# The first feed-forward product with 512 columns instead of 480, the last 32 zeros

## The chip, the cores and the metric

The kernel runs on one core of one Trainium2 chip. The metric is the device time of one execution in microseconds (us); of the kernel before there are two runs, 1797.93 and 1798.88 us, with a median of 1798.41 us. Engines are named as the profile names them: PE is TensorE (PEld its weight loads), DVE is VectorE, ACT is ScalarE, POOL is GpSimd, SP is SyncE.

## The reference

```
x: (4, 12480, 128)   inducing: (32, 128)   w_in: (128, 2048)   w_out: (2048, 128)
def mab(q, kv):
    s = scale * (q @ kv.T);  s = s - s.max(-1)
    a = exp(s);  a /= a.sum(-1) + 1e-9
    return a @ kv
h = mab(inducing, x)             # per batch: 32 rows, from all 12480 tokens
y = mab(x, h)                    # each token over those 32 rows
r = max(y @ w_in, 0)
out = (r * r) @ w_out            # (49920, 128)
```

Two attentions per batch, and then a feed-forward with a squared ReLU. The bulk of the arithmetic is the feed-forward: 49,920 tokens through 128 x 2048 and 2048 x 128.

## The kernel before

**Tiling.** A batch has 13 units of 960 tokens, and a unit has two blocks of 480 tokens (`BLK`). The feed-forward runs block by block. Its 2048 hidden features are 16 tiles of 128, taken as 8 pairs, so there are 4 x 13 x 2 x 8 = 832 pairs in all.

**One pair.** `wide` (L508) makes the hidden features: two products, one for each tile of the pair, each with a weight tile of 128 x 128 (from `hw`, which is h @ w_in, made once per batch) and with `st` as the streamed operand. `st` holds the unnormalised attention weights of the block's 480 tokens, split into a high and a low part, on 128 partitions. The two results lie in `hp`, a PSUM tile of two banks of 512 float32 each, of which columns 0 to 479 are written. ACT reads those 480 columns of both banks (`relu`, L515, into `r`) and squares them (`square`, L522, into `g`). DVE or POOL rounds `g` to the shorter format fp32r (`high`, through `copy`, L593 or L595, into `hi`), and DVE subtracts (`low`, L530, into `lo`). Then `narrow` (L543) adds six products of 480 columns to the block's result `op`: hi with wo_hi, hi with wo_lo, lo with wo_hi, for both tiles. In one pair of each unit (marked "f" in the table `HI`) there is no split; it has two products in full float32 (`wo_f` with `g`). Both operands of `wide` are fp32r, as are those of the six narrow products.

**What makes `st`.** `second_unit` computes the second attention of the unit that comes next. Its last steps, `back(k)` (L477: four small products into a PSUM bank `ap`) and `stacked(k)` (L483 to L486), give `st` for block k: for k = 0 ACT copies `ap` to `st`, for k = 1 DVE does. `st` has four buffers. The other matrix work on PE is the first attention of the next batch (`xtp`, `sp`, `ep`, `hp` at L324), the scores (`s`, `s2t`) and the transposes of the output (`otp`).

**Order.** Nothing is scheduled by the tool chain: every step is put on one list with a position in time (`at(t, fn)`, the clock being pairs), the list is sorted, and the steps are emitted in that order. So each engine's queue follows the positions written in the kernel, and every engine takes its queue in order. POOL's queue holds the roundings `hi` that the table `HI` gives it (five in a unit), and three steps on `sk` (the split of the attention weights), of which the last copies the low part.

Of the kernel before, what the change touches and what calls it, by code (L numbers as in the profile page):

```python
# [11 lines left out]
F32 = mybir.dt.float32  # L12
F32R = mybir.dt.float32r
# [5 lines left out]
PSUM = bass.MemoryType.PSUM  # L19

P = 128
TS = 120          # tokens of a sub-tile
NT = 8            # sub-tiles of a unit
UNIT = TS * NT    # tokens of a unit
BLK = UNIT // 2   # tokens of a block, the width of the feed-forward products


@with_exitstack
def induced_attention_then_squared_relu_ffn(
# [8 lines left out]
    nc = tc.nc  # L38
    B, N, C = x.shape
# [3 lines left out]
    NP = NF // 2  # L43
    NU = N // UNIT
    Q = P // M
    scale = 1.0 / math.sqrt(C)
    # engines, by pair of f-tiles in the first and the second block of a unit; "f": not split
    SQ = ('aaaaaaaa', 'aaaaaaaa')   # of the square
    HI = ('vpvpvvpf', 'vvpvvpvv')   # of the rounding
    # engines that empty PSUM  # L50
    XT, XT_EARLY, ET, SS, ST, OT = 'av', 'aa', 'a', 'v', 'av', 'vv'
    RB, GB, HB, LB = 3, 4, 4, 3
    AT_G1, AT_SQA, AT_SQV, AT_HIP, AT_HIA, AT_HIV, AT_LO, AT_G2, AT_G2D = -1.4, 1.05, 0.8, 1.1, 0.7, 1.2, 2.05, 3.3, 0.16
# [17 lines left out]
    att = ctx.enter_context(tc.tile_pool(name="att", bufs=2))  # L71
# [5 lines left out]
    def bank(name):  # L77
        return ps_m.tile([P, 512], F32, tag="m", name=name)

    # token p * (N / TS) + j of a batch lies on partition p of sub-tile j  # L80
    x_v = x.rearrange("b (p j) c -> b p j c", p=TS)
    out_v = out.rearrange("(b p j) c -> b p j c", b=B, p=TS)

    def load_x(b, u, pool):
        xn = pool.tile([TS, NT, C], F32, tag="xn", name=f"xn_{b}_{u}")
        nc.sync.dma_start(xn, x_v[b, :, u * NT:(u + 1) * NT, :])
        return xn
# [4 lines left out]
    make_identity(nc, ident)  # L92
    identr = const.tile([P, P], F32R, name="identr")
    nc.vector.tensor_copy(identr, ident)
    # same_m[(q m), (k m')] = (m == m')
    same_m = const.tile([P, Q, M], F32, name="same_m")
    nc.vector.tensor_reduce(
        same_m[:, 0, :], ident.rearrange("p (q m) -> p m q", q=Q), axis=AX.X, op=ALU.add
# [2 lines left out]
        nc.vector.tensor_copy(same_m[:, k, :], same_m[:, 0, :])  # L101

    same = same_m.rearrange("p k m -> p (k m)")
    # lane_q[(q m), q'] = (q == q')
    lane_q = const.tile([P, Q], F32, name="lane_q")
    nc.vector.tensor_reduce(
        lane_q, ident.rearrange("p (q m) -> p q m", q=Q), axis=AX.X, op=ALU.add
# [6 lines left out]
    indT = const.tile([C, M], F32, name="indT")  # L114
    nc.vector.tensor_copy(indT, it_ps[:C, :M])

# [1 line left out]
    plan = []  # L118

    def at(t, fn):  # L120
        plan.append((t, len(plan), fn))
# [1 line left out]
    w_in_sb = const.tile([C, F], F32, name="w_in_sb")  # L123
    wo_hi = const.tile([P, NF, C], F32R, name="wo_hi")
    wo_lo = const.tile([P, NF, C], F32R, name="wo_lo")
    # w_out's tiles for the products that are not split
    FULL = [p for p in range(NP) if "f" in (HI[0][p], HI[1][p])]
    wo_f = const.tile([P, 2 * max(len(FULL), 1), C], F32, name="wo_f")

# [3 lines left out]
    ABOVE = float(np.array(1151 << 20, np.int32).view(np.float32))  # L133

    def weights(name, load, use, t0, step):
        """Steps that turn float64 weights, as words (low, high), into float32 parts (a, b).

        a has the leading 21 bits and b the rest; what float32 has no exponent for becomes 0 or
        infinite, as a cast would have it: a high word's order as a float32 is that of its exponent.
        """  # L140
        v = {}
        shape = [P, WCH]

        def tile_of(tag, dtype):
            return pools["stage"].tile(shape, dtype, tag=tag, name=f"{tag}_{name}")

        def words():
            v["w"] = pools["stage"].tile([P, WCH, 2], I32, tag="words", name=f"words_{name}")
            load(v["w"])

        def clamp():
            v["hc"] = tile_of("hc", F32)
            nc.vector.tensor_scalar(
                v["hc"], v["w"][:, :, 1].bitcast(F32), ABOVE, -ABOVE, ALU.min, ALU.max
            )

        def size():
            v["m"] = tile_of("m", F32)
            nc.scalar.activation(v["m"], v["hc"], AF.Abs)

        def flush():
            nc.vector.scalar_tensor_tensor(v["hc"], v["m"], LEAST, v["hc"], ALU.is_ge, ALU.mult)

        def field():
            v["a"] = tile_of("a", I32)
            nc.vector.tensor_scalar(
                v["a"], v["hc"].bitcast(I32), 3, 0x3FFFFFF8,
                ALU.logical_shift_left, ALU.bitwise_and,
            )

        def sign():
            nc.vector.scalar_tensor_tensor(
                v["a"], v["hc"].bitcast(I32), -0x40000000, v["a"], ALU.bitwise_and, ALU.bitwise_or
            )

        def power():
            v["power"] = tile_of("m", I32)
            nc.vector.tensor_single_scalar(v["power"], v["a"], -0x800000, ALU.bitwise_and)

        def low():  # L180
            v["b"] = tile_of("b", F32)
            nc.vector.scalar_tensor_tensor(
                v["b"], v["w"][:, :, 0].bitcast(U32), 2.0 ** -52, v["power"].bitcast(F32),
                ALU.mult, ALU.mult,
            )
            use(v["a"].bitcast(F32), v["b"])

        at(t0 - 1.5, words)
        for i, fn in enumerate((clamp, size, flush, field, sign, power, low)):
            at(t0 + step * i, fn)  # L190
# [4 lines left out]
        pools["stage"] = pools["scope"].enter_context(tc.tile_pool(name="stage", bufs=2))  # L195

    def open_ffn():
        """The feed-forward takes the place of the weights' staging."""
        pools["scope"].close()
        pools["ffn"] = ctx.enter_context(tc.tile_pool(name="ffn", bufs=3))  # L200

# [38 lines left out]

    state = {}

# [1 line left out]
    # lane (q m): inducing point m over the sub-tiles 2q and 2q + 1 of each unit  # L244
    def first_unit(b, u, t0, ahead, times, early=False):
        v = {}
        n = f"{b}_{u}"
        s = state.setdefault(b, {"xt": []})
# [4 lines left out]
        def turn(k):  # L253
# [8 lines left out]
            for t in range(4):  # L262
                nc.tensor.transpose(  # L263
                    tp[:, t * TS:(t + 1) * TS], v["xn"][:, 4 * k + t, :], ident[:TS, :TS]
                )
# [19 lines left out]
            nc.vector.tensor_reduce(v["mx"], v["sp"][:, :2 * TS], axis=AX.X, op=ALU.max)  # L285

        def shift():
            # the maximum so far, times -scale
            v["neg"] = tiny.tile([P, 1], F32, tag="neg", name=f"neg_{n}", bufs=4)
            if u:  # L290
                v["before"] = s["neg"]
                nc.vector.scalar_tensor_tensor(
                    v["neg"], v["mx"], -scale, s["neg"], ALU.mult, ALU.min
                )
            else:
                nc.vector.tensor_scalar_mul(v["neg"], v["mx"], -scale)
            s["neg"] = v["neg"]
# [50 lines left out]
            at(t0 + t, fn)  # L348

    def first_end(b, t0, times):  # L350
        """Joins the lanes of each inducing point; h transposed, four times, and h @ w_in split."""
        v = {}
        s = state[b]

# [50 lines left out]
        for t, fn in zip(times, fns):  # L405
            at(t0 + t, fn)

# [1 line left out]
    def second_unit(b, u, t0, times):  # L409
        """The unnormalised weights of a unit's tokens, split in two, as (hi, lo, hi, lo) on partitions."""  # L410
        v = {}
        n = f"{b}_{u}"
        s = state[b]
# [67 lines left out]
                )  # L481

        def stacked(k):  # L483
            st = att.tile([P, BLK], F32R, tag="st", name=f"st_{n}_{k}", bufs=4)
            copy(ST[k], st, v["ap"][:, :BLK])
            s["st", u, k] = st  # L486

        fns = (
# [3 lines left out]
        for t, fn in zip(times, fns):  # L492
            at(t0 + t, fn)

# [1 line left out]
    def ffn_block(b, u, k, t0):  # L496
        n = f"{b}_{u}_{k}"
        s = state[b]
        w = {}

        def pair(p):
            v = {}

            def wide(i):
                if i == 0:
                    v["hp"] = ps_h.tile([P, 2, 512], F32, tag="h", name=f"h_{n}_{p}")
                f = 2 * p + i
                nc.tensor.matmul(  # L508
                    v["hp"][:, i, :BLK], s["hw"][:, f * P:(f + 1) * P], s["st", u, k],
                    start=True, stop=True,  # L510
                )

# [60 lines left out]
        def turned():  # L573
            if k == 0:
                s["osb", u] = att.tile([TS, NT, C], F32, tag="osb", name=f"osb_{b}_{u}")
            # block k holds the sub-tiles 2q + k
            nc.vector.tensor_mul(  # L577
                s["osb", u].rearrange("t (q k) c -> t k q c", k=2)[:, k],
                w["tp"][:TS, :].rearrange("t (q c) -> t q c", q=Q),
                s["zz", u][:, k * Q:(k + 1) * Q].broadcast_to([TS, Q, C]),  # L580
            )
            if k == 1:
                nc.sync.dma_start(out_v[b, :, u * NT:(u + 1) * NT, :], s["osb", u])

# [4 lines left out]
    def copy(engine, dst, src):  # L589
        if engine == "a":  # L590
            nc.scalar.copy(dst, src)  # L591
        elif engine == "v":
            nc.vector.tensor_copy(dst, src)  # L593
        else:
            nc.gpsimd.tensor_scalar(dst, src, 1.0, 0.0, ALU.mult, ALU.add)  # L595

    # batch 0's first attention, then per batch its blocks and the first attention of the next
    U = 2 * NP
    t_end = START * NU + T_END
    t_main = t_end + T_FFN  # L600
# [52 lines left out]
```

## Time and profile before

| | |
|---|---|
| time, two runs | 1797.93 and 1798.88 us, median 1798.41 |
| span of the profiled execution | 1796.8 us; the runs' times are 1.1 to 2.1 us above it |
| mean granted clock of PE | 0.994 |
| PE busy | 1766.7 us, 98% |
| ACT busy | 1628.0 us, 91% |
| DVE busy | 1620.0 us, 90% |
| POOL busy | 442.8 us, 25% |
| share of PE in the chain that ended last | 95% |

The profiled execution's own time is not given apart from its span; its time lies with the two runs, its span plus one or two microseconds. In the page, a group row has the line, the engine, the operation, the operands with shapes, the count, then busy time and mean duration in ns, and the idle time of the engine before it. The rows of the timeline and of the chain begin with the start in us and the duration in us; "x2" means that two instructions are merged in the row. PE's durations contain the passage through the array, which overlaps the next product: what a product costs is read from the distance between starts. A float32 product appears as two records with the same operands, so the two float32 products of each of the 52 units are 208 records.

### The profile page before, as it was taken

What the parts mean: (1) busy time and instruction counts of PE and PEld (TensorE: products, weight loads), DVE (VectorE), ACT (ScalarE), POOL (GpSimd) and SP (SyncE); (2) the same over time, 40 slices, a digit from 0 to 9 for tenths busy, and PEclk for the clock granted to TensorE, in tenths of its full rate; (3) what the DMA queues carried; (4) which work ended last, traced back from release to release, by engine and by line L of the source; (5) the groups of instructions that cost most, each with busy time, mean ns of one, the idle gap of its engine ahead of it and who ended that gap; (6) DMA issues with size and microseconds to landing.
All of it is one profiled execution on the core that took longest, in us unless ns stands there. A gap on an engine that the chain in (4) does not pass through costs nothing.

```text
span 1796.8 us, 27067 instructions
## 1 busy us (share of the span) xinstructions
PE 1766.7 (98%) x9729; PEld 1422.9 (79%) x9729; DVE 1620.0 (90%) x2315; ACT 1628.0 (91%) x2070; POOL 442.8 (25%) x439
## 2 busy tenths in 40 slices
PE   7799999999999999999999999999999999999998
PEld 4478888888778888888878888888887888888887
DVE  6899989999989989989989989989989999999998
ACT  5699999999899999999988999999999999999997
POOL 1312222222222222222221222222222323233231
PEclk9899999999999999999999999999999999999999
DMA  8200100100100110100100110110100000000000
GB/s 214 57 23 23 44 23 23 45 23 23 45 23 23 37 31 23 45 23 23 45 23 23 28 39 23 35 33 23 38 19 12 23 12 23 12 16 19 12 23 23
DMA packets 16912, 57.07 MB, mean 32 GB/s; under 512 B 1704, under 2 KB 3784, under 8 KB 16776
## 3 DMA queue, kind: packets, MB, share of 16 engines
q1 hardware_dynamic: 16776, 55.34, 11.5%
q8 instruction: 76, 1.25, 0.3%
q14 instruction: 60, 0.49, 0.1%
HBM read 29.77 MB, written 25.56 MB: 31 GB/s over the span
## 4 chain that ended last, share of the span: by engine, by line
PE 95%; DVE 2%; DMA 1%; issue 0%; ACT 0%; SPq 0%; POOL 0%; ACTq 0%; DVEq 0%
PE op L543 62%; PE h L508 20%; PE otp L569 3%; PE ap L477 2%; PE xtp L263 2%; PE s L420 2%; PE hp L324 1%; PE sp L278 1%; PE wp L393 1%; DMA words_i<-in_moe_w_in_dram 1%; PE s2t L432 1%; DMA words_o<-in_moe_w_out_dram 1%; PE ep L312 1%; DVE lo L530 0%; DVE mx L285 0%
## 5 line engine op out<-in xcount | busy, mean ns | idle before, releaser
L530 DVE TENSOR_TENSOR lo<-g,hi 128x960 fp32r<-128x960 f32 x780 | 941.9, 1214 | 68.6 <-POOL hi L595 39.1
L515 ACT ACTIVATE r<-h 128x960 f32<-128x960 f32 x832 | 812.0, 976 | 96.8 <-PE h L508 93.7
L522 ACT ACTIVATE g<-r 128x960 f32<-128x960 f32 x832 | 839.6, 1009 | 0.0
L595 POOL TENSOR_SCALAR hi<-g 128x960 fp32r<-128x960 f32 x260 | 282.8, 1088 | 1112.0 <-ACT g L522 1058.1
L543 PE MATMUL op<-hi,wo_hi 128*128 128x480 f32 x1560 | 520.1, 407 | 0.0
L508 PE MATMUL h<-st,hw 128*128 128x480 f32 x1664 | 507.7, 386 | 0.0
L543 PE MATMUL op<-lo,wo_hi 128*128 128x480 f32 x1560 | 479.4, 383 | 0.0
L543 PE MATMUL op<-hi,wo_lo 128*128 128x480 f32 x1560 | 476.2, 381 | 0.0
L593 DVE CAST hi<-g 128x960 fp32r<-128x960 f32 x520 | 374.1, 719 | 3.4 <-ACT g L522 3.4
L543 PEld LDWEIGHTS op<-hi,wo_hi 128*128 128x128 f32 x1560 | 284.4, 189 | 91.7 <-issue 58.7
L508 PEld LDWEIGHTS h<-st,hw 128*128 128x128 f32 x1664 | 306.1, 189 | 47.7 <-issue 3.9
L543 PEld LDWEIGHTS op<-hi,wo_lo 128*128 128x128 f32 x1560 | 293.7, 188 | 43.6
L543 PEld LDWEIGHTS op<-lo,wo_hi 128*128 128x128 f32 x1560 | 293.5, 188 | 41.4 <-DVE lo L530 0.2
L595 POOL TENSOR_SCALAR sk<-d 120x256 fp32r<-120x256 f32 x104 | 102.5, 1001 | 86.3 <-ACT d L446 86.3
L593 DVE COPY ot<-op 128x480 f32<-128x480 f32 x104 | 67.9, 653 | 59.8 <-PE op L543 59.7
L543 PE MATMUL op<-g,wo_f 128*128 128x480 f32 x208 | 100.7, 565 | 0.0
L477 PEld LDWEIGHTS ap<-identr,sk 120*128 120x128 f32 x416 | 62.9, 192 | 26.2 <-issue 20.0
L477 PE MATMUL ap<-identr,sk 120*128 120x120 f32 x416 | 76.3, 306 | 2.0 <-POOL sk L595 2.0
L577 DVE TENSOR_TENSOR osb<-otp,zz 120x512 f32<-120x512 f32 x104 | 70.7, 680 | 2.9 <-PE otp L569 2.2
L263 PE MATMUL xtp<-ident,xn 120*128 120x120 f32 x416 | 63.9, 279 | 8.2 <-DMA xn<-in_x_dram 4.0
L263 PEld LDWEIGHTS xtp<-ident,xn 120*128 120x128 f32 x416 | 51.2, 147 | 22.3 <-ACT xt L591 5.1
L569 PE MATMUL otp<-ident,ot 128*120 128x128 f32 x416 | 63.8, 276 | 0.8 <-DVE ot L593 0.8
(89 smaller groups left out, 867.3 us busy)
## 6 DMA issues: line engine op xcount, KB each, us to landing
xn<-in_x_dram SPq DMA_DIRECT2D x52, 480.0 KB, 5.7
out_dram<-osb SPq DMA_DIRECT2D x52, 480.0 KB, 3.7
words_i<-in_moe_w_in_dram SPq DMA_DIRECT2D x4, 512.0 KB, 6.7
words_o<-in_moe_w_out_dram SPq DMA_DIRECT2D x4, 512.0 KB, 5.0
ind_sb<-in_inducing_dram SPq DMA_DIRECT2D x1, 16.0 KB, 1.7
```

The source lines that it names most:

```text
L263: nc.tensor.transpose(tp[:, t * TS:(t + 1) * TS], v["xn"][:, 4 * k + t, :], ident[:TS, :TS])
L420: nc.tensor.matmul(sp[q * M:(q + 1) * M, :2 * TS], s["hT"][:, :M], xt[:, q * 2 * TS:(q + 1) * 2 * TS], start=True, stop=True,)
L477: nc.tensor.matmul(ap[:, q * TS:(q + 1) * TS], v["sk"][:, k * Q + q].rearrange("t a k m -> t (a k m)"), identr[:TS, :TS], start=(q == 0), ...
L508: nc.tensor.matmul(v["hp"][:, i, :BLK], s["hw"][:, f * P:(f + 1) * P], s["st", u, k], start=True, stop=True,)
L515: nc.scalar.activation(v["r"], v["hp"][:, :, :BLK], AF.Relu)
L522: nc.scalar.activation(v["g"], v["r"], AF.Square)
L530: nc.vector.tensor_sub(v["lo"], v["g"], v["hi"])
L543: nc.tensor.matmul(w["op"][:, :BLK], wo[:, f, :], v[part][:, i, :], start=(p == 0 and j == 0), stop=(p == NP - 1 and j == len(steps) - 1),)
L569: nc.tensor.transpose(tp[:TS, q * P:(q + 1) * P], w["ot"][:, q * TS:(q + 1) * TS], ident)
L577: nc.vector.tensor_mul(s["osb", u].rearrange("t (q k) c -> t k q c", k=2)[:, k], w["tp"][:TS, :].rearrange("t (q c) -> t q c", q=Q), s["zz ...
L593: nc.vector.tensor_copy(dst, src)
L595: nc.gpsimd.tensor_scalar(dst, src, 1.0, 0.0, ALU.mult, ALU.add)
```

## The change

`st` becomes a tile of 512 columns. In `stacked`, before the copy, GpSimd sets its last 32 columns to zero, and the copy writes the first 480 as before. `wide` streams all 512 columns, so its result fills both banks of `hp`. `relu` and everything behind it reads columns 0 to 479 as before, so the last 32 columns of `hp` are read by nobody. The rest of the diff removes comments; lines behind L484 shift by one.

```
-            st = att.tile([P, BLK], F32R, tag="st", name=f"st_{n}_{k}", bufs=4)
-            copy(ST[k], st, v["ap"][:, :BLK])
+            st = att.tile([P, 512], F32R, tag="st", name=f"st_{n}_{k}", bufs=4)
+            nc.gpsimd.memset(st[:, BLK:].bitcast(F32), 0.0)
+            copy(ST[k], st[:, :BLK], v["ap"][:, :BLK])
             s["st", u, k] = st
...
-                    v["hp"][:, i, :BLK], s["hw"][:, f * P:(f + 1) * P], s["st", u, k],
+                    v["hp"][:, i, :], s["hw"][:, f * P:(f + 1) * P], s["st", u, k],
                     start=True, stop=True,
```

On POOL, in the middle of a unit of the first batch, this stands in a row before; `sk` is the split attention weight of the unit to come, `hi` a rounding of the unit that runs (its numbers are unit, block and pair), and the brackets name the engines whose counters the instruction waits for:

```order
L595 TENSOR_SCALAR hi_3_0_6_2233<-g_3_0_6_2230 128x960 [waits PE_49,Activation_49]
L595 TENSOR_SCALAR sk_4_2188<-sk_4_2188 120x8x32 [waits DVE_49]
L595 TENSOR_SCALAR hi_3_1_2_2328<-g_3_1_2_2326 128x960 [waits PE_49,Activation_49]
L595 TENSOR_SCALAR hi_3_1_5_2406<-g_3_1_5_2403 128x960 [waits DVE_49,PE_49,Activation_49]
L595 TENSOR_SCALAR hi_4_0_1_2487<-g_4_0_1_2484 128x960 [waits PE_49,Activation_49]
```

The same place with the change:

```order
L596 TENSOR_SCALAR hi_3_0_6_2241<-g_3_0_6_2238 128x960 [waits PE_49,Activation_49]
L596 TENSOR_SCALAR sk_4_2196<-sk_4_2196 120x8x32 [waits DVE_49]
L485 MEMSET st_4_0_2308 128x32
L596 TENSOR_SCALAR hi_3_1_2_2337<-g_3_1_2_2335 128x960 [waits PE_49,Activation_49]
L485 MEMSET st_4_1_2352 128x32
L596 TENSOR_SCALAR hi_3_1_5_2416<-g_3_1_5_2413 128x960 [waits DVE_49,PE_49,Activation_49]
L596 TENSOR_SCALAR hi_4_0_1_2497<-g_4_0_1_2494 128x960 [waits PE_49,Activation_49]
```

Two instructions a unit are added, 104 in all, one ahead of the rounding of pair 2 of the second block and one ahead of that of pair 5; neither waits for another engine, and the order of the others is as before.

On PE, at the first feed-forward products of the program, this stands before (`wp` is a product that makes `hw`, `xtp` a transpose of the next batch's tokens):

```order
L393 MATMUL wp_3_922<-w_in_sb,hT_863 128x512 [waits DVE_49]
L508 MATMUL h_0_0_0_924<-st_0_0_920,hw_865 128x480 [waits Activation_49]
L508 MATMUL h_0_0_0_924<-st_0_0_920,hw_865 128x480
L263 MATMUL xtp_0_0_930<-ident,xn_0_787 128x120 [waits DMAHW5_49,PE_49]
L263 MATMUL xtp_0_0_930<-ident,xn_0_787 128x120 x3
L508 MATMUL h_0_0_1_935<-st_0_0_920,hw_865 128x480 x2
```

And with the change:

```order
L393 MATMUL wp_3_923<-w_in_sb,hT_863 128x512 [waits DVE_49]
L509 MATMUL h_0_0_0_925<-st_0_0_920,hw_865 128x512 [waits Activation_49,Pool_49]
L509 MATMUL h_0_0_0_925<-st_0_0_920,hw_865 128x512
L263 MATMUL xtp_0_0_931<-ident,xn_0_787 128x120 [waits DMAHW5_49,PE_49]
L263 MATMUL xtp_0_0_931<-ident,xn_0_787 128x120 x3
L509 MATMUL h_0_0_1_936<-st_0_0_920,hw_865 128x512 x2
```

All 1664 wide products stream 512 columns. Their order is unchanged; the first one of each of the four batches now waits for POOL too, and the others carry no such wait. ACT and DVE have the same instructions, order and waits as before.

## The prediction

> **What bounds the kernel now.** I read the page's first part and its chain of waits, then busy time by stage, then the timeline of a stretch without attention work.
>
> ```profile
> span 1796.8 us, 27067 instructions
> PE 1766.7 (98%) x9729; PEld 1422.9 (79%) x9729; DVE 1620.0 (90%) x2315; ACT 1628.0 (91%) x2070; POOL 442.8 (25%) x439
> PE 95%; DVE 2%; DMA 1%; issue 0%; ACT 0%; SPq 0%; POOL 0%; ACTq 0%; DVEq 0%
> ```
>
> The chain that ended last is 95% PE. A busy PE alone would not say that PE is the bound, since the durations contain the passage through the array; the chain does, because it follows releases. Where PE is not busy, by stage (start and end in us, then the busy time of each engine):
>
> ```profile
> 0.00:60.00 60.00, 40.94 (x453) 27.72 (x457) 42.59 (x110) 33.36 (x90) 15.20 (x17) 0.90 0.78 202
> 60.00:100.00 40.00, 36.00 (x193) 24.40 (x189) 29.72 (x52) 31.82 (x47) 11.82 (x14) 0.90 0.00 1
> 100.00:500.00 400.00, 399.38 (x2219) 321.31 (x2212) 365.70 (x518) 366.97 (x467) 93.11 (x96) 1.00 0.11 30
> 500.00:1000.00 500.00, 499.35 (x2777) 401.51 (x2776) 455.16 (x646) 458.25 (x580) 117.98 (x121) 1.00 0.11 29
> 1000.00:1400.00 400.00, 400.00 (x2191) 323.07 (x2192) 365.74 (x519) 368.67 (x466) 93.45 (x96) 1.00 0.10 27
> 1400.00:1797.00 397.00, 391.07 (x1913) 324.91 (x1911) 361.10 (x475) 368.92 (x425) 111.26 (x97) 1.00 0.07 18
> ```
>
> PE's idle time is 23 us in the first 100 us, where weights are loaded and the first attention runs, and 6 us in the last stage, mostly the output's end. From 100 to 1400 us it is 1.3 us of 1300 us. There is no slack there into which a longer product could go. The granted clock is 1.00 there.
>
> The pace, from the chain in order of time (start, duration, piece), with a last row from the end of the kernel:
>
> ```profile
> 909.91 0.43 PE h L508 x2
> 910.34 1.32 PE op L543 x6
> 911.66 0.43 PE h L508 x2
> 912.09 1.32 PE op L543 x6
> 913.41 0.43 PE h L508 x2
> ...
> 1782.98 7.45 PE op L543 x34
> ```
>
> A pair takes 911.66 - 909.91 = 1.75 us for eight products of 480 columns, 0.219 us each; 34 narrow products at the end take 7.45 us, 0.219 us each as well, with nothing else to do. By the pieces a wide product takes 0.43 / 2 = 0.215 us and a narrow one 1.32 / 6 = 0.22: about the same. ACT is nearly as full: in these pairs
>
> ```profile
> 909.75:911.50 1.75, 1.75 (x10) 1.51 (x8) 1.75 (x3) 1.75 (x3) 1.75 (x1) 1.00 0.00 0
> ACT r L515 <- PE h L508: 93.7, 182, 0.9
> PEld h L508 <- issue: 3.9, 14, 0.5
> ```
>
> it is busy 1.75 of 1.75 us (fourth engine column). But over the span it is ACT that waits for the wide products (93.7 us, 182 times). The longest wait seen ahead of their weight loads is 3.9 us of issue, which is none for ACT. PE leads and ACT follows closely; a slower PE makes ACT's waits longer and starves nobody that is on the path.
>
> **The change: 32 columns more in 1664 products.** Order, count and operands of all other products stay. What a column costs is the one number that matters, and before there is no wide product of 512 columns. Rows near it are the float32 products, whose two records start one after the other, at 480 columns (wo_f) and 512 columns (wp):
>
> ```profile
> 1005.66 0.57 PE L543 MATMUL op<-g,wo_f 128*128 128x480 f32 x1
> 1006.06 0.57 PE L543 MATMUL op<-g,wo_f 128*128 128x480 f32 x1
> ...
> 484.37 0.59 PE L393 MATMUL wp<-w_in_sb,hT 128*128 128x512 f32 x1
> 484.80 0.59 PE L393 MATMUL wp<-w_in_sb,hT 128*128 128x512 f32 x1
> ```
>
> 0.40 us for 480 columns and 0.43 for 512: 0.83 and 0.84 ns per column, so time in proportion to columns, and no step at a full bank. An fp32r product with its 0.219 us per 480 cannot pay 0.83 ns per column; it is consistent with half of it, 0.417 ns, which makes 0.200 us for 480 and leaves 0.019 us whose cause I don't know. If the 0.019 us is fixed per product, 32 columns cost 32 x 0.417 = 13.3 ns. If it is part of the streaming, they cost 32 x 219/480 = 14.6 ns. Those are the ends of the likely case. I take 14 ns, between them, since no row parts them.
>
> How many of the 1664 are on the path? By the chain's shares by line,
>
> ```profile
> PE op L543 62%; PE h L508 20%; PE otp L569 3%; PE ap L477 2%; PE xtp L263 2%; PE s L420 2%; PE hp L324 1%; PE sp L278 1%; PE wp L393 1%; DMA words_i<-in_moe_w_in_dram 1%; PE s2t L432 1%; DMA words_o<-in_moe_w_out_dram 1%; PE ep L312 1%; DVE lo L530 0%; DVE mx L285 0%
> ```
>
> L508 has 20% of 1796.8 = 359 us, and 1664 x 0.219 = 364 us: all but a few. The term is 1664 x 14 ns = 23.3 us (22.1 to 24.3). PE's idle time from 100 us on, 7 us, most of it in the tail behind the last wide product, could swallow at most 1 or 2 us of it. I leave 0.7 us for that: **+22.6 us**.
>
> The Trainium skill's page "TensorE: Matmul & The Clock Gate" (section "Wait — 56ns, not 53.3ns?") has back-to-back products start N / 2.4 GHz + 2.5 ns apart at full clock, which is 202.5 ns at 480 columns and 215.8 ns at 512. Its difference is the same 13.3 ns, and by it the sum would be 22.2 us; but its 202.5 ns is not what this trace has at 480 columns, 0.219 us, and for 512 it gives less than that. That is a case of its own, the first rival below.
>
> **The zeros.** 104 memsets of 128 x 32 on POOL. The nearest rows are the two sizes of memset in the setup:
>
> ```profile
> masks.py:197 POOL MEMSET ident<- 128x128 f32 x1 | 0.2, 205 | 0.3 <-POOLq L636 0.3
> L636 POOL MEMSET const-float32-0.0<- 128x1 f32 x1 | 0.1, 98 | 0.2 <-issue 0.2
> ```
>
> So each costs between 98 and 205 ns, about 0.12 us, 12 us in all on an engine that is 25% busy. They stand in POOL's queue ahead of two roundings, in this stretch of POOL's timeline behind the 0.41 us row and behind the first 0.99 us row:
>
> ```profile
> 1002.00 0.41 POOL L595 TENSOR_SCALAR sk<-sk 120x256 fp32r<-120x256 f32 x1 [2.19 <-DVE z L453]
> 1008.18 0.99 POOL L595 TENSOR_SCALAR hi<-g 128x960 fp32r<-128x960 f32 x1 [5.77 <-ACT g L522]
> 1013.72 0.99 POOL L595 TENSOR_SCALAR hi<-g 128x960 fp32r<-128x960 f32 x1 [4.54 <-ACT g L522]
> ```
>
> POOL waits 5.77 and 4.54 us there for ACT's square, so memsets that wait for nobody are over long before: cost 0. If that cover were gone, each would delay a rounding, the subtraction and the products behind it by 0.1 to 0.2 us, 10 to 21 us in all. The products that read the zeros come a block later or more, except at the start of a batch; there the wait for POOL is new, four times, and bounded by one memset each, below 1 us together. What goes on beside a memset on DVE could be slowed; DVE's chain share is 2% and the memsets add up to 12 us, so 0 to 1 us, taken as 0. ACT and DVE copy the same 480 columns to `st` as before, and `relu` reads the same columns.
>
> **Sum.** 1796.8 + 22.6 = 1819.4 us of span; the runs' median is 1.6 us above the profiled span, so **1821 us**, 1.2 to 1.3% above 1798.4.
>
> **The rivals.**
>
> *Hidden columns.* The 0.219 us are set not by the stream but by something that goes on beside it, and 512 columns, 0.215 us by half of the float32 row's 0.43, fit under it. Then the time stays 1798 us. For it: the spacing is 0.019 us above half of the float32 row's, and a weight load takes most of it,
>
> ```profile
> L508 PEld LDWEIGHTS h<-st,hw 128*128 128x128 f32 x1664 | 306.1, 189 | 47.7 <-issue 3.9
> 901.04 0.42 PEld L477 LDWEIGHTS ap<-identr,sk 120*128 120x128 f32 x3 [0.21 <-issue]
> ```
>
> 189 of 219 ns. Against: in the second row three loads of the same number of columns lie within 0.42 us; with the last as long as the 0.19 us of the first row, they start 0.115 us apart, with a product of 120 columns behind each. A load so does not need 0.219 us. The page's 215.8 ns at 512 columns says the same thing as this rival: what keeps 480 columns from 202.5 ns could be there still, and swallow the difference. Between this and my forecast lies a partial case, where the excess of 19 ns shrinks as the stream grows: 3 to 8 ns per product, 1803 to 1812 us.
>
> *The full float32 price* (the other side, slower by over 2%). An fp32r column beyond the 480th pays 0.83 ns, as the float32 rows do, because a result that fills its bank leaves no pause between one product and the next. 32 x 0.83 = 26.7 ns, x 1664 = 44 us: 1843 us. It passes 2% from 36.0 / 1664 = 21.6 ns per product on. Against: the float32 row at a full bank (0.43) has no such step.
>
> *Memsets in the way.* A memset holds up POOL's rounding or DVE by its whole length, 10 to 21 us beside the 22.6: 1831 to 1842. Against: the 4.5 to 5.8 us of idle time quoted above.
>
> *A gain.* A full-width product goes faster than one of 480, at 0.215 instead of 0.219 us: 1664 x -4 ns = -7 us, 1791 us. No row speaks for it but the excess that I can't explain. That the change does nothing is ruled out by the built program, in which all 1664 products have 512 columns.
>
> **Numbers.** Forecast 0.70 (its own range 1816 to 1825 us), partial 0.08, hidden 0.14, full float32 price 0.04, memsets 0.02, gain 0.02. From 1802 to 1826, the forecast and the partial case hold 0.78, so the range goes on to the hidden case: 1797 to 1826 us. Over 2% (about what a measurement of this kernel tells from no change; below 1762 or above 1834 us): faster 0.01, slower 0.05, within 0.94.
>
> **What would show it.** In the changed profile two wide products should take 0.46 to 0.47 us in the chain instead of 0.43, six narrow ones still 1.32; a pair 1.78 us; L508's share of the chain (now L509) 21%; ACT's wait for the wide products up from 93.7 us by something near 20 us; the memsets 0.1 to 0.2 us each with POOL's long waits for the square behind them. Wide pairs still at 0.43 to 0.44 us would be the hidden case; narrow products that also become slower, or a new wait of DVE for POOL beyond its present kind, would show that the sum lacks a term.

## The result, and the profile after

The median is 1824.82 us (two runs, 1824.39 and 1825.24) against 1798.41 before: 26.4 us more, a ratio of 1.0145 with a 95% interval of 1.0125 to 1.0164. The forecast was 1821 us. The change is within 2% of before, and the interval leaves out 1, so the loss is clear of the noise. The profiled execution has a span of 1823.1 us and a time of 1825.24 us.

The page of the changed kernel, first part, chain by engine and line, and two groups:

```profile
span 1823.1 us, 27175 instructions
PE 1791.4 (98%) x9729; PEld 1422.9 (78%) x9729; DVE 1612.2 (88%) x2315; ACT 1634.0 (90%) x2070; POOL 454.4 (25%) x543
...
PE 95%; DVE 2%; DMA 1%; issue 1%; POOL 0%; SPq 0%; ACT 0%; POOLq 0%; DVEq 0%
PE op L544 61%; PE h L509 21%; PE otp L570 3%; PE ap L477 2%; PE xtp L263 2%; PE s L420 1%; PE hp L324 1%; PE sp L278 1%; DMA words_i<-in_moe_w_in_dram 1%; PE wp L393 1%; PE s2t L432 1%; PE ep L312 1%; DVE lo L531 0%; DMA words_o<-in_moe_w_out_dram 0%; DVE mx L285 0%
...
L516 ACT ACTIVATE r<-h 128x960 f32<-128x960 f32 x832 | 813.4, 978 | 114.8 <-PE h L509 109.0
L509 PE MATMUL h<-st,hw 128*128 128x512 f32 x1664 | 531.8, 401 | 0.0
```

PE is still the chain. Its busy time grew by 24.7 us, nearly all of it in the wide products: from 507.7 us, in this row of the kernel before, to 531.8 us (L509, above). ACT's wait for them grew from 93.7 to 109.0 us.

```profile
L508 PE MATMUL h<-st,hw 128*128 128x480 f32 x1664 | 507.7, 386 | 0.0
```

Busy time by stage, with the change:

```profile
100.00:500.00 400.00, 399.38 (x2198) 317.66 (x2197) 358.61 (x513) 363.08 (x456) 94.20 (x115) 1.00 0.11 30
500.00:1000.00 500.00, 499.41 (x2725) 394.67 (x2724) 444.37 (x637) 452.66 (x574) 118.25 (x148) 1.00 0.10 29
1000.00:1400.00 400.00, 400.00 (x2164) 318.07 (x2163) 356.76 (x512) 364.46 (x459) 96.64 (x119) 1.00 0.10 28
```

PE has no more idle time than before; what fell is the number of products done in the same time (2725 in place of 2777 between 500 and 1000 us). The chain in order of time, for two pairs and at the end:

```profile
921.07 0.46 PE h L509 x2
921.53 1.31 PE op L544 x6
922.84 0.46 PE h L509 x2
923.30 1.31 PE op L544 x6
924.61 0.47 PE h L509 x2
...
1809.23 7.50 PE op L544 x34
```

A pair takes 1.77 us in place of 1.75. The two wide products went from 0.43 to 0.46 or 0.47, the six narrow ones from 1.32 to 1.31. POOL's timeline over a place where both zeros stand:

```profile
1015.69 0.41 POOL L596 TENSOR_SCALAR sk<-sk 120x256 fp32r<-120x256 f32 x1 [1.42 <-DVE z L453]
1016.03 0.12 POOL L485 MEMSET st<- 128x32 f32 x1
1022.32 0.99 POOL L596 TENSOR_SCALAR hi<-g 128x960 fp32r<-128x960 f32 x1 [6.16 <-ACT g L523]
1023.25 0.12 POOL L485 MEMSET st<- 128x32 f32 x1
1027.85 0.99 POOL L596 TENSOR_SCALAR hi<-g 128x960 fp32r<-128x960 f32 x1 [4.47 <-ACT g L523]
```

The memsets take 0.12 us each, and behind them POOL waits 6.16 and 4.47 us for ACT.

### The profile page after: what moved, and what is told of

It is laid out like the page before. It is cut to its first block, busy times and chain, and to the rows that moved or that the text cites. A ratio compares the mean times of both kernels' runs of the same rounds, so it can differ in the third digit from the quotient of the medians.

```text
span 1823.1 us, 27175 instructions
## 1 busy us (share of the span) xinstructions
PE 1791.4 (98%) x9729; PEld 1422.9 (78%) x9729; DVE 1612.2 (88%) x2315; ACT 1634.0 (90%) x2070; POOL 454.4 (25%) x543
## 4 chain that ended last, share of the span: by engine, by line
PE 95%; DVE 2%; DMA 1%; issue 1%; POOL 0%; SPq 0%; ACT 0%; POOLq 0%; DVEq 0%
PE op L544 61%; PE h L509 21%; PE otp L570 3%; PE ap L477 2%; PE xtp L263 2%; PE s L420 1%; PE hp L324 1%; PE sp L278 1%; DMA words_i<-in_moe_w_in_dram 1%; PE wp L393 1%; PE s2t L432 1%; PE ep L312 1%; DVE lo L531 0%; DMA words_o<-in_moe_w_out_dram 0%; DVE mx L285 0%
## 5 line engine op out<-in xcount | busy, mean ns | idle before, releaser
L531 DVE TENSOR_TENSOR lo<-g,hi 128x960 fp32r<-128x960 f32 x780 | 958.5, 1235 | 73.1 <-PE op L544 31.3
L516 ACT ACTIVATE r<-h 128x960 f32<-128x960 f32 x832 | 813.4, 978 | 114.8 <-PE h L509 109.0
L596 POOL TENSOR_SCALAR hi<-g 128x960 fp32r<-128x960 f32 x260 | 286.9, 1104 | 1147.3 <-ACT g L523 1068.1
L509 PE MATMUL h<-st,hw 128*128 128x512 f32 x1664 | 531.8, 401 | 0.0
L594 DVE CAST hi<-g 128x960 fp32r<-128x960 f32 x520 | 349.7, 672 | 2.9 <-ACT g L523 2.8
L509 PEld LDWEIGHTS h<-st,hw 128*128 128x128 f32 x1664 | 306.8, 189 | 47.5 <-issue 4.1
L596 POOL TENSOR_SCALAR sk<-d 120x256 fp32r<-120x256 f32 x104 | 97.8, 956 | 90.7 <-ACT d L446 90.7
```

The lines of the kernel that those rows point to most:

```text
L509: nc.tensor.matmul(v["hp"][:, i, :], s["hw"][:, f * P:(f + 1) * P], s["st", u, k], start=True, stop=True,)
L516: nc.scalar.activation(v["r"], v["hp"][:, :, :BLK], AF.Relu)
L531: nc.vector.tensor_sub(v["lo"], v["g"], v["hi"])
```

## The experiments

In what follows, *spacing* is the distance between the starts of the first and the second wide product of a pair in the trace, as a mean over the 726 to 738 of 832 pairs in which it is below 250 ns. The others follow a transpose, a float32 product or a product of the attentions, behind which the first record starts too early to tell the distance. *Stretch* is the time from the start of the first wide product to that of the last; it leaves out the beginning and the tail. Before: spacing 217.9 ns, stretch 1712.6 us. With the change: 232.3 ns and 1737.9 us. The stretch differs by some 2 us between executions of the same products: with the zeros alone (below), where PE has the same products as before, it is 1710.4 us.

My theory was that each of the 1664 wide products pays for its 32 columns on PE and the zeros cost nothing. The rivals were that the zeros have a share in it, that the price is a step at a full bank, and that columns are hidden. What remained open inside the theory was whether an fp32r product's time goes by columns wholly, or has a fixed part.

**The zeros alone.** `st` has 512 columns and gets its zeros, but the product streams 480:

```
-  v["hp"][:, i, :], s["hw"][:, f * P:(f + 1) * P], s["st", u, k],
+  v["hp"][:, i, :BLK], s["hw"][:, f * P:(f + 1) * P], s["st", u, k][:, :BLK],
```

> The zeros alone: st has 512 columns and GpSimd sets the last 32, but the first feed-forward product streams 480 as before. My sum (columns cost, memsets hidden): as before, 1798 us within 1 us, wide products again 0.215 to 0.219 us apart. Rival (the memsets hold up POOL's roundings or DVE): some of the 26.4 us stays; the part that the wider products don't explain by their spacing (26.4 - 1664 x 14.8 ns = 1.8 us) or more, 1800 us and up.

1795.95 us against 1797.92 of before on the same chip, ratio 0.999 (0.9981 to 1.0). Spacing 217.8 ns. The memsets are there and cost nothing:

```profile
L485 POOL MEMSET st<- x104: 117/124/634, 67.1 to 1746.0; 128x32 f32 x104
L509 PE MATMUL h<-st,hw 128*128 128x480 f32 x1664 | 507.4, 386 | 0.0
```

(The first row has the shortest, the median and the longest duration in ns.) The time is 2 us under the expectation, so their price is nil, and the rival that they share in the 26.4 us falls.

**512 columns without the 104 memsets.** Four fixed tiles, zeroed once at the start:

```
+    st_fixed = [const.tile([P, 512], F32R, name=f"stf{i}") for i in range(4)]
+    for st in st_fixed:
+        nc.gpsimd.memset(st[:, BLK:].bitcast(F32), 0.0)
...
-            st = att.tile([P, 512], F32R, tag="st", name=f"st_{n}_{k}", bufs=4)
-            nc.gpsimd.memset(st[:, BLK:].bitcast(F32), 0.0)
+            st = st_fixed[2 * ((b * NU + u) % 2) + k]
```

> 512 columns without the 104 memsets: st is one of four fixed tiles whose last 32 columns are zeroed once at the start. My sum: as with the change, 1824 to 1825 us, since the columns are the whole price. Rival (memsets share in it): 1823 us or less, by what the memsets cost.

1825.16 us, ratio 1.0146 (1.0129 to 1.0163), the same as the change itself; spacing 232.1 ns, stretch 1738.4 us. Two wide products take 0.47 us in the chain here too:

```profile
915.36 0.47 PE h L511 x2
915.83 1.24 PE op L546 x4
917.07 0.47 PE h L511 x2
917.54 1.31 PE op L546 x6
```

With the run before it, the whole of the loss lies in the columns.

**496 columns.** Half of the added columns; from the changed kernel:

```
-  v["hp"][:, i, :], s["hw"][:, f * P:(f + 1) * P], s["st", u, k],
+  v["hp"][:, i, :496], s["hw"][:, f * P:(f + 1) * P], s["st", u, k][:, :496],
```

> The wide product streams 496 columns, 16 of them zeros. If the price goes by column (13.3 to 14.8 ns per 32): 11 to 13 us above before, 1809 to 1812 us, wide products 0.224 to 0.225 us apart. If it is a step at a full bank of 512: as before, 1798 us. If products are rounded up to the next 32 or 64 columns: the whole 26 us, 1824 us.

1811.41 us, ratio 1.0073 (1.0058 to 1.0088): 13.5 us above before, half of the change's 26.4, and the stretch is 12.7 us longer, half of 25.4. The page's group and the chain:

```profile
L509 PE MATMUL h<-st,hw 128*128 128x496 f32 x1664 | 517.7, 392 | 0.0
...
915.15 0.45 PE h L509 x2
915.60 1.30 PE op L544 x6
916.91 0.45 PE h L509 x2
```

0.45 us for two, between the 0.43 of before and the 0.46 to 0.47 of the change. Neither a step at a full bank nor a rounding up to 512 gives this (steps of 16 columns or fewer would look the same). The spacing was 224.6 ns, as expected of a price by column.

**416 columns.** The other way, from the kernel before. The last 64 columns of `hp` hold the zeros of two fixed PSUM tiles, so those tokens' features are left out:

```
-  v["hp"][:, i, :BLK], s["hw"][:, f * P:(f + 1) * P], s["st", u, k],
+  v["hp"][:, i, :416], s["hw"][:, f * P:(f + 1) * P], s["st", u, k][:, :416],
```

> The other way: the wide product streams 416 columns, 64 fewer (the last 64 tokens of each block are left out of it and get what the two fixed, once zeroed PSUM tiles hold; ACT and all others read 480 columns as before). Spacing of the wide products: 0.191 us if the excess of 0.019 us is fixed and a column costs 0.417 ns; 0.1885 us if all of it goes by columns (0.453 ns). Time: if PE alone were the bound, 1664 x 29 ns = 48 us less, 1750 us; if ACT, busy all of the 1.75 us of a pair without attention work, takes over at once, little is gained and it stays above 1780 us.

1757.88 us in one run, 40 us less than before. ACT did not take over, as I had thought possible: it still waits 62.0 us for the wide products, and PE's share of the chain stays:

```profile
PE 95%; DVE 2%; DMA 1%; issue 0%; ACT 0%; SPq 0%; POOL 0%; ACTq 0%; DVEq 0%
...
ACT r L523 <- PE hf L516: 62.0, 160, 0.7
```

The spacing is 191.0 ns, 26.9 ns less for 64 columns. Of the 1664 x 27 ns = 45 us the stretch kept 41.1; where the rest went is not shown.

The kernel so is PE-bound on both sides of 480 columns. The two expectations for the spacing (0.191 and 0.1885) lie too near to each other: the first product's distance fits the one with the fixed part, that from the second wide product to the narrow one behind it, 188.6 ns, the other. A wider range was needed, and the mean of the two distances, 189.8 ns, is read again below.

**Narrow products of 256 columns.** From the kernel before; the sums of the last 224 tokens of a block get only their first term:

```
-                    w["op"][:, :BLK], wo[:, f, :], v[part][:, i, :],
+                    w["op"][:, :(BLK if p == 0 and j == 0 else 256)], wo[:, f, :],
+                    v[part][:, i, :(BLK if p == 0 and j == 0 else 256)],
```

> Separates the two readings of the 0.017 us that an fp32r product takes beyond 0.417 ns per column: every narrow product but a block's first streams 256 of its 480 columns (the sums for the other 224 tokens of a block stay at their first term). If all goes by columns (0.4525 ns): narrow products 0.116 us apart. If a fixed 0.0165 to 0.0185 us comes on top of 0.417 ns per column: 0.123 to 0.125 us. Three weight loads with short products in the trace of before lay 0.115 us apart, so nothing below that is expected. Time: PE alone would save 4576 x about 0.094 = 430 us; ACT, busy 1628 us in the span, must take over long before that: 1650 to 1700 us.

Between narrow products in a row (a distance counted where it and the one before it are undisturbed, 1672 of them) the mean is 117.6 ns: near the 116 of a price by column, and not the 123 to 125 of a fixed part. But it also lies near the 115 ns at which loads follow each other, which may hold it up. The time was 1678.28 us. ACT is nearly full there (889 of the 900 us from 100 to 1000 us), but the chain, contrary to the expectation, is DVE's:

```profile
DVE 65%; PE 13%; ACT 11%; issue 8%; POOL 1%; DMA 1%; DVEq 0%; SPq 0%; ACTq 0%; POOLq 0%
DVE lo L530 37%; DVE hi L594 14%; ACT g L522 6%; PE op L543 5%; ACT r L515 4%; PE h L508 3%; DVE osb L578 3%; PE s L420 1%; DVE xt L594 1%; DVE d L443 1%; PE xtp L263 1%; DVE sk L469 1%; DVE mx L439 1%; DVE z L450 1%; DVE zs L337 1%
```

**Narrow products of 336 columns.** The same edit with 336, clear of that floor:

> Every narrow product but a block's first streams 336 of 480 columns (the sums of the last 144 tokens of a block stay at their first term), far enough above the 0.115 us at which weight loads follow each other. If the time of an fp32r product goes by columns (0.4525 ns): 0.152 us apart. If 0.0165 to 0.0185 us are fixed: 0.1565 to 0.1585 us.

Two products take 0.31 us in this stretch of PE's timeline:

```profile
910.92 0.47 PE L543 MATMUL op<-hi,wo_lo 128*128 128x336 f32 x2
911.23 0.47 PE L543 MATMUL op<-lo,wo_hi 128*128 128x336 f32 x2
911.54 0.47 PE L543 MATMUL op<-hi,wo_hi 128*128 128x336 f32 x2
```

The mean is 153.3 ns (1814 distances), against 152 expected of a price by column and 156.5 to 158.5 of a fixed part. In the kernel before, the narrow products counted in the same way lie 218.2 ns apart. So 336 columns cost 0.456 ns each and 480 cost 0.455; the slope between them is 64.9 / 144 = 0.451 ns, which leaves 2 ns that don't go by columns. A fixed part of 16.5 to 18.5 ns falls for this range: the time of an fp32r product here goes by its columns, at 0.45 ns. The other widths lie within 2.3 ns of the same line: by it 256 columns take 117.2 ns, 416 take 189.4, 496 take 225.4 and 512 take 232.6. Measured were 117.6 and, as the mean of the two distances of a wide pair, 189.8, 223.1 and 232.0. So nothing shows that the loads held up the 256 columns. The time was 1673.2 us, with DVE in the chain:

```profile
DVE 77%; issue 8%; ACT 8%; PE 4%; DMA 2%; DVEq 0%; POOL 0%; SPq 0%; ACTq 0%; POOLq 0%
```

**A load of 96 columns of weights.** Why 0.45 and not the 0.417 ns of half a float32 product? One suspect is the weight load that runs beside each stream. Here the wide product has 96 columns of weights; the last 32 features of each tile are left out:

```
-  v["hp"][:, i, :BLK], s["hw"][:, f * P:(f + 1) * P], s["st", u, k],
+  v["hp"][:96, i, :BLK], s["hw"][:, f * P:f * P + 96], s["st", u, k],
```

> Is the excess of 0.017 us the weight load that runs beside the stream? The wide product loads 96 columns of weights instead of 128 and streams 480 (the last 32 hidden features of each tile are left out; ACT reads the zeros of fixed PSUM tiles there). If the load takes its share from the stream, the excess falls by a quarter, the product that runs beside a load of 96 columns is 0.213 us from the next (the narrow one ahead of the pair and the first of the pair) and the others stay at 0.217. If not, all stay at 0.217 us and the time at 1798 us.

The load became shorter, 162 in place of 189 ns, and the product did not:

```profile
L516 PEld LDWEIGHTS hf<-st,hw 128*96 128x96 f32 x1664 | 263.6, 162 | 67.4 <-issue 3.7
L516 PE MATMUL hf<-st,hw 128*96 128x480 f32 x1664 | 507.1, 386 | 0.4 <-DVE hf L248 0.4
```

1801.09 us in one run (before, on that chip: 1799.39), spacing 219.6 ns; the distance from the narrow product ahead to the first wide one, beside whose stream a short load runs, was 217.6 ns, against 218.2 before. The spacing behind the first product of the pair rose a little and the other fell a little, where 213 ns had been expected of both. So a load that is 27 ns shorter does not change the pace.

**bf16 operands in the wide product.** `st` and `hw` in bf16, which rounds them more coarsely; nothing is left out. One kernel with 480 columns, from the kernel before, and one with 512, from the changed one:

```
-            s["hw"] = hw_pool.tile([P, F], F32R, tag="hw", name=f"hw_{b}")
+            s["hw"] = hw_pool.tile([P, F], BF16, tag="hw", name=f"hw_{b}")
...
-            st = att.tile([P, BLK], F32R, tag="st", name=f"st_{n}_{k}", bufs=4)
+            st = att.tile([P, BLK], BF16, tag="st", name=f"st_{n}_{k}", bufs=4)
```

> Is the excess of 0.017 us one of the format? st and hw are bf16 (rounded further than the reference allows for; nothing left out), so the wide product has bf16 operands, 480 columns. If the excess belongs to fp32r operands or their weight loads: wide products 0.200 to 0.203 us apart, 1664 x 15 ns = 25 us less, 1773 us. If it belongs to any product that is followed by another's weight load: 0.217 us as before, 1798 us.

> The same with 512 columns, zeros by GpSimd as in the change. In both cases 32 columns should add 13.3 ns per wide product, 22 us: 0.214 to 0.216 us apart and 1795 us if the excess is one of fp32r, 0.231 us and 1820 us if not.

One run each gave 1783.38 and 1804.48 us, between the two expectations. With four and five runs:

> The bf16 wide product of 480 columns once more, timed in rounds: 1783 us in one look, 16 us under before. If that is the format's price it stands: ratio 0.991.

> The bf16 wide product with 512 columns, timed beside the one of 480. If a column costs 0.417 ns in bf16: 22.2 us above it. If 32 columns cost what they cost in fp32r by the timed change (26.4 us / 1664 = 15.9 ns): 26 us above it.

480 columns: 1782.16 us, ratio 0.991 (0.9895 to 0.9925). 512 columns: 1805.62 us, ratio 1.0039 (1.0025 to 1.0054). So the format is worth 16.8 us / 1664 = 10 ns per product at 480 columns, and 32 columns cost 23.5 us / 1664 = 14.1 ns in bf16 by the time, 12.9 by the stretch (1695.9 and 1717.4 us). The spacing is 211.7 ns at 480 columns (830 pairs) and 224.9 at 512 (673 pairs; this trace lacks a tenth of the wide products), 13.2 ns apart. By the traces, then, a column costs about 0.41 ns in bf16, not 0.45, and by the spacing what lies above 0.417 ns per column is 11.7 ns at 480 columns and 11.6 at 512: here it does not grow with the columns. The pairs in the chain of the two timed kernels:

```profile
909.56 0.42 PE h L509 x2
...
911.74 0.42 PE h L509 x2
```

```profile
910.25 0.45 PE h L510 x2
...
914.91 0.45 PE h L510 x2
```

Their weight loads are half as long (98 ns in place of 189, page of the first bf16 kernel):

```profile
L509 PEld LDWEIGHTS <-hw 128*128 128x128 bf16 x1664 | 103.4, 98 | 179.7 <-issue 166.7
```

Part of what a product takes above 0.417 ns per column then comes with the fp32r operands or their longer loads: at 480 columns about 10 of 17 ns by the time, 6 by the spacing. What the rest is, and by what mechanism fp32r is slower, stays open. The bf16 kernel with 480 columns is the one version here that computes the whole result and is clearly faster than both kernels, by 0.9% against before, at the price of the coarser rounding.

## Why the prediction was right, point by point

**The bound.** PE was the bound, and the time followed it in both directions: +13.5 us at 496 columns, +26.4 at 512, -40 at 416. The reading that carried this was the stage row with 1.3 us of idle time in 1300, along with ACT's 93.7 us of waiting for the wide products. That ACT was busy 1.75 of 1.75 us in a pair did not make it a second bound at 416 columns; I had left that open, and it falls for that width.

**The term of the columns** was right in kind and a little small in size. I took 14 ns, from the ends 13.3 and 14.6. By the spacing the first product of a pair pays 232.3 - 217.9 = 14.4 ns, and the second one (its distance to the narrow product) 231.7 - 216.5 = 15.2 ns. By the stretch it is 25.4 us / 1664 = 15.2 ns, against the 23.3 us of the sum. The upper end, 14.6 ns from 219/480 per column, was the better reading: nearly all of the 0.019 us that I could not place goes by columns, as 336 columns showed. What was off in size is so the choice of the middle "since no row parts them", by 0.4 to 1.2 ns per product, about 2 us by the stretch. That lies near the 2 us by which the stretch differs between executions, so the spacing shows the direction and the stretch does not settle the amount.

**The 0.7 us that idle time would swallow** did not show: the stretch grew by more than the products' spacing gives (1664 x 14.8 ns = 24.6 us). The span is 26.3 us longer against the 22.6 of the sum; of these 3.7 us, 2.1 are the columns, 0.7 this term, and the remaining 0.9 lie in the beginning. The first wide product started 0.9 us later than before, at 70.9 in place of 70.0 us. With the zeros alone it started at 68.9 and with 496 columns at 69.6, so the beginning varies by a microsecond or two between executions; I don't put this on the change. The time of 1824.82 us came in just under the upper end of the forecast's own range, 1816 to 1825, so that the number held is in part luck.

**The zeros** cost nothing, as the sum had it: 0.12 us each by the trace, which is the estimate, behind waits of 6.16 and 4.47 us. The kernel with the zeros alone settles it, and with it the rival of the memsets (0.02).

**Hidden columns** (0.14) and the **partial case** (0.08) are refuted by 496 and 512 columns. Their argument, that something beside the stream holds a product at 0.219 us, was tried at its likeliest suspect: a weight load shorter by 27 ns changes nothing. The Trainium skill's page "TensorE: Matmul & The Clock Gate" (section "Wait — 56ns, not 53.3ns?") has back-to-back products start N / 2.4 GHz + 2.5 ns apart at full clock; the estimate worked out from it is 202.5 ns at 480 columns and 215.8 at 512, a difference of 13.3 ns. The distances here, 217.9 and 232.3 ns for the first product of a pair, agree with the difference within one to two nanoseconds (14.4 and 15.2) and with neither value: fp32r products lie 15 to 17 ns above them. In bf16 the difference was 12.9 to 14.1 ns, and the spacing, 211.7 and 224.9 ns, lies 9 ns above them.

**The full float32 price** (0.04) would have been 26.7 ns per product; 15.2 is its refutation. **The gain** (0.02) is refuted by the sign.

**What would show it.** Wide pairs at 0.46 to 0.47 us, narrow ones unchanged, L509 at 21% of the chain, memsets of 0.12 us: all came. The pair took 1.77 us, not 1.78, and ACT's wait grew by 15 us, not 20. DVE's wait before the subtraction came under another name. Before:

```profile
DVE lo L530 <- POOL hi L595: 39.1, 45, 1.0
```

With the change:

```profile
DVE lo L531 <- PE op L544: 31.3, 33, 1.0
DVE lo L531 <- POOL hi L596: 12.9, 15, 1.2
```

The waits are about as many (45, then 33 + 15) and together a little longer (39.1, then 44.2 us). So this is for the most part the wait that was there, in which the narrow products that free the buffer `lo` now come last more often than POOL's rounding. It is 39.0 us for POOL with the zeros alone and 12.5 us with 512 columns and no memsets in the loop, so it comes with the columns and not with the memsets. Why the order turns is not shown: at 496 columns, where PE is slower too, the wait for POOL is still 40.2 us. The chain's share of DVE stays at 2%.

## What to carry to other kernels

Where the chain is one engine and a stage row shows it without idle time, a longer instruction on it cost its added length times its count here, and nothing hid it, though another engine was nearly as full. Price a column from the spacing of the same format in the same trace, and where a spacing is larger than a neighbouring format suggests, measure a second width before deciding whether the excess is fixed: in fp32r it grew with the columns here, and in bf16, by the spacing, it did not. Padding a product to a whole bank was no gain here and had no step; small memsets on an engine that waits several microseconds for its next input were free here.

## What the runs showed of the hardware that I had not expected

The time of an fp32r product goes by its columns at about 0.45 ns (153.3 ns at 336, 217.9 at 480, 232.3 at 512) while the float32 records lie at 0.83 to 0.84 ns per column, which is not twice that. Going to bf16 in the wide product saves 10 ns of 217 per product by the time, with loads half as long, while a load shorter by 27 ns within fp32r saves nothing.

With 256 columns in the narrow products ACT's instructions became longer, from 976 and 1009 to 1105 and 1145 ns, with the same shapes:

```profile
L522 ACT ACTIVATE g<-r 128x960 f32<-128x960 f32 x832 | 952.4, 1145 | 0.0
L515 ACT ACTIVATE r<-h 128x960 f32<-128x960 f32 x832 | 919.6, 1105 | 5.0 <-PE h L508 4.5
```

and that kernel was slower (1678.28 us) than the one with 336 columns (1673.2 us, 1031 and 1070 ns). I don't know why; each is a single run.
